# A table of priorities found offline, last rows kept in the score banks, last sums in two steps, and early memory denominators in a fused attention and MLP kernel

## The chip, the cores and the metric

The kernel runs on one core of one Trainium2 chip. The metric is the device time of one execution in microseconds (us), as the median of several runs. The profile of one execution is also at hand. In before its span, from the first to the last instruction, was 274.2 us, 1.7 us shorter than the device time of that same execution (275.94). A run is called slow here when it is over 1.5% above the fastest run of the same kernel.

## The reference, cut to what matters

```python
x = A_x                                   # (1, 2048, 512), bf16
xn = layernorm(x)
return x + A(xn, wq, wk, wv, wo, beta) + B(xn, w1, w2)

def B(x, w1, w2):                         # 512 -> 1792 -> 512
    return silu(x @ w1) @ w2

def A(x, wq, wk, wv, wo, beta):           # 32 heads of 16, 4 segments of 512 rows
    q, k, v = ...                         # split into heads and segments
    g = sigmoid(beta)
    M, z = 0, 0
    for s in range(4):
        p = softmax(qs @ ks.T * scale + causal_mask)
        a_dot = p @ vs
        pq = phi(qs)                      # phi(t) = t + 1 if t > 0 else exp(t)
        a_mem = (pq @ M) / (pq @ z + 1e-6)
        outs.append(g * a_mem + (1 - g) * a_dot)
        pk = phi(ks)
        M, z = M + pk.T @ vs, z + sum(pk)
    return concat(outs) @ wo
```

Two things can be divided late. A probability row is divided by its sum after it has been multiplied by the values, and `a_mem` is divided by its own denominator. In this kernel both kinds of denominator travel: they are gathered into a small tile, inverted by VectorE, written to DRAM, and read back as a full "replica" tile that VectorE multiplies with.

## The kernel before

The kernel is written as a plan. Each operation has an engine, a duration, a latency, dependencies and a due time, all in nanoseconds. A list scheduler, run while the kernel is built, simulates the five engines with these durations. The order that it finds is the order in which each engine gets its instructions.

```python
def op(self, eng, occ, lat, fn, due, r=(), w=(), kind="", take=None, ...):
    ...                                     # o.due = due, written by hand: tau(n) = T0 + n * PER
# in schedule(): per engine, the ready operation with the smallest key
key = -1e9 if o.kind in ("S",) else o.due   # score tiles first, then by due time
if o.kind == "PV" and lastS:
    key = -1e8
```

The first loads are such operations too. Their latency is a constant, whatever else is moving:

```python
load([("wk",)], ld_w("wk", "A_wk"), 2, 4000)      # keys, function, due, latency
load([("wq",)], ld_w("wq", "A_wq"), 3, 5000)
load([("wv",)], ld_w("wv", "A_wv"), 4, 6000)
load([("w1",)], ld_w("w1", "B_w1"), 5, 11000)
...
load([("w2",)], ld_w("w2", "B_w2"), 8, 16500)
```

Attention has 4 segments of 4 groups of 8 heads, and 5 score tiles for each group. That makes 80 score tiles, which all pass through one tile of four banks:

```python
for dt in range(DT):                        # 4 groups in a segment
    for q in range(5):
        op("PE", 222, 215, sc, tau(n) - 700, ..., w=[("psS", n)], kind="S")     # scores into psS
        op("ACT", 1757, 170, ex, tau(n) - 5000, r=[("psS", n)], w=[("Pt", n, 0)], kind="exp")
        op("POOL", ..., mask, ...)          # causal mask
    pvo = op("PE", 1090, 215, pv, tau(n0 + 8), ..., kind="PV")                   # probabilities x values
    ...                                     # evictions, row sums to zf, merge of two halves
```

At the end of each segment one `norm` handles the denominators of all four groups and of the memory together, and `out` makes the rows. Each row tile takes 14 matmuls with `w2`, evicted by VectorE together with x, then 4 with `wo`, evicted again. These groups share four banks `psb` with everything except the scores.

```python
def rc(K):                                  # after the sums of all 4 groups have landed
    K.nc.vector.reciprocal(out=K.rec32[lo:P, :], in_=K.zf[i2][lo:P, :])
    K.nc.vector.tensor_scalar(out=K.rec[i2][lo:P, :], in0=K.rec32[lo:P, :], scalar1=K.gcol[lo:P, 0:1], ...)
```

The softmax here doesn't subtract the row's maximum and nothing guards it: scores larger than these inputs give would overflow.

Of the kernel before, what the change touches and what calls it, by code (L numbers as in the profile page):

```python
# [9 lines left out]
ALU = mybir.AluOpType  # L10
# [21 lines left out]
PER = 2450  # L32
NB = 4
WARM = 60

RING = dict(
    xnT=2, kT=6, kTo=6, qT=6, phiK=1, phiQ=6, V=6, Pt=8, th=2, N=5, No=2, oT=4,
    zf=2, rec=2, rep=6, x=3, ek=3, phiKT=2, xn=2, pq=2, at=2, mv=4, rstd=4, zc=2,
    Mbf=2, zden=2, xa=4, stats=3, psS=1, drec=4, M32=1, z32=1,
# [12 lines left out]

def mm_ns(n):
    return n / 2.4 + 2.6


class Op:
    __slots__ = (
        "eng", "occ", "lat", "deps", "fn", "due", "kind", "take", "free", "mode",
        "start", "done", "bank", "n", "nleft", "outs", "hold", "not_before", "soft", "after",  # L60
    )


class Plan:

    def __init__(self):
        self.ops = []
        self.acc = {}
        self.build()
        self.link()  # L70
        self.schedule()

    def op(self, eng, occ, lat, fn, due, r=(), w=(), kind="", take=None, free=(), mode="F",
           deps=(), hold=0, not_before=0, after=()):
        o = Op()
        o.eng, o.occ, o.lat, o.fn, o.due, o.kind = eng, occ, lat, fn, due, kind
        o.take, o.free, o.mode = take, free, mode
        o.hold, o.not_before = hold, not_before
        o.deps = set(deps)
        o.n = len(self.ops)  # L80
        o.after = after
        o.outs = []
        o.start = o.done = None
        for k in r:
            self.acc.setdefault(k, ([], []))[0].append(o)
        for k in w:
            self.acc.setdefault(k, ([], []))[1].append(o)
        self.ops.append(o)
        return o
# [53 lines left out]
    def gemm(self, name, n, lhsT, rhs, due, r, ncol=L, extra=0):  # L143
        t = {}
        last = None
        for i in range(n):
            def fn(K, i=i):
# [6 lines left out]
                deps=[last] if last else (),  # L154
# [3 lines left out]
    def build(self):  # L158
# [24 lines left out]
        load([("wk",)], ld_w("wk", "A_wk"), 2, 4000)  # L183
        load([("wq",)], ld_w("wq", "A_wq"), 3, 5000)
        load([("wv",)], ld_w("wv", "A_wv"), 4, 6000)
        load([("w1",)], ld_w("w1", "B_w1"), 5, 11000)
        load([("x", 1, 0)], ld_x(1, 0), 6, 11500)
        load([("x", 1, 1)], ld_x(1, 1), 7, 12000)
        load([("w2",)], ld_w("w2", "B_w2"), 8, 16500)
        load([("wo",)], ld_w("wo", "A_wo"), 9, 17500)  # L190

        def beta(K):
            for r0, r1, ap in ((0, 64, [[0, 2], [1, 32], [1, 1]]), (64, P, [[1, 32], [0, 2], [1, 1]])):
                K.nc.sync.dma_start(
                    out=K.bcol[r0:r1, :],
                    in_=bass.AP(tensor=K.A_beta.tensor, offset=K.A_beta.offset, ap=ap),
                )
        op("SP", 1050, 2300, beta, 30000, w=[("bcol",)], kind="load", not_before=14000)
        for s in range(2, NSEG):
            for h in range(2):  # L200
                load([("x", s, h)], ld_x(s, h), 40000 + 1000 * s + h, 2600, nb=16000)
# [3 lines left out]
        def lnc(K):  # L205
            K.nc.gpsimd.memset(K.lnc[:, :, 0:1], EPS)
            K.nc.gpsimd.memset(K.lnc[:, :, 1:2], -0.5)
# [15 lines left out]
        def bmask(K):  # L223
# [12 lines left out]
            K.nc.gpsimd.memset(K.half[0:64, :], 0.5)  # L236
            K.nc.gpsimd.memset(K.half[64:128, :], -0.5)
            K.nc.gpsimd.memset(K.z32[:], 0.0)
        op("POOL", 2200, 150, bmask, 35000, w=[("bmask",), ("half",)], not_before=16000)

        def gate(K):
            K.nc.scalar.activation(out=K.gcol[:], in_=K.bcol[:], func=AF.Tanh, scale=K.half[:, 0:1])
            K.nc.vector.tensor_scalar(
                out=K.gcol[:], in0=K.gcol[:], scalar1=1.0, scalar2=None, op0=ALU.add
            )
        op("ACT", 300, 400, gate, 36000, r=[("bcol",), ("half",)], w=[("gcol",)])
# [22 lines left out]
    def ln(self, s, tau):  # L269
        op = self.op  # L270
        base = 1000 if s == 0 else (tau(1) if s == 1 else tau(20 * (s - 1) - 8))
        for j in range(TPS):
# [6 lines left out]
            op("DVE", 662, 150, stats, base + 700 * j, r=[("x", s, j // 2)],  # L279
               w=[("mv", s, j), ("stats", t)])  # L280
        step = 2 if s else 2
        for h in range(0, TPS, step):
            def rstd(K, h=h):
                t0 = s * TPS + h
                rs = K.rstd[:, t0 : t0 + step, :]
                K.nc.gpsimd.tensor_tensor(
                    out=rs, in0=K.mv[:, t0 : t0 + step, 1:2], in1=K.lnc[:, 0:step, 0:1], op=ALU.add
                )
                K.nc.gpsimd.tensor_tensor(out=rs, in0=rs, in1=K.lnc[:, 0:step, 1:2], op=ALU.pow)
            op("POOL", 770, 150, rstd, base + 1500 + 700 * h,  # L290
               r=[("mv", s, h + i) for i in range(step)] + [("lnc",)], w=[("rstd", s, h // step)])
        for j in range(TPS):
            t = s * TPS + j

            def norm(K, j=j, t=t):
# [5 lines left out]
            op("DVE", 300, 130, norm, base + 2000 + 700 * j,  # L301
               r=[("x", s, j // 2), ("mv", s, j), ("rstd", s, j // step)], w=[("xn", t)])
            if s == 0:
# [9 lines left out]
                op("PE", 420, 215, tr, base + 2500 + 700 * j, r=[("xn", t), ("ident",)],  # L313
# [18 lines left out]
    def proj(self, s, tau):  # L332
# [4 lines left out]
        for dt in range(DT):  # L337
            due = tau(20 * s + 5 * dt) - 3500
# [14 lines left out]
            op("POOL", 655, 130, odd, due + 1800, r=[("kT", 4 * s + dt), ("pm",)], w=[("kTo", 4 * s + dt)])  # L353
            if s < NSEG - 1:
# [4 lines left out]
                    tau(20 * s + 5 * dt + 4), lambda K, dt=dt: K.zc[i2][:, dt : dt + 1],  # L359
# [7 lines left out]
                op("SP", 1220, 2200, trk, tau(20 * s + 5 * dt + 6), r=[("phiKT", g)],  # L367
# [10 lines left out]
            if s > 0:  # L378
# [3 lines left out]
                    tau(20 * s + 2 + 2 * dt), None, [],  # L382
                )
        for j in range(TPS):
            due = tau(20 * s + 6) - 3500 + 100 * j
# [12 lines left out]
    def phi(self, s, dt, skey, src, dkey, dst, due, acc, extra):  # L398
# [19 lines left out]
        op("DVE", 690 if acc else 605, 140, st, due, r=[skey, ("ek", g, 1), ("ek", g, 0)],  # L418
           w=[dkey] + extra)

    def w1(self, s, tau):
# [3 lines left out]
        for ft in range(FT):  # L425
            g = s * FT + ft
            due = tau(2 + g * 74 / 56)
# [19 lines left out]
    def attend(self, s, tau):  # L447
# [9 lines left out]
        def p_ap(K, n0, par, g, kt):  # L457
            pt = lambda q: K.Pt[(n0 + q) % RING["Pt"]]
# [6 lines left out]
        for dt in range(DT):  # L465
            n0 = 20 * s + 5 * dt
            for q in range(5):
                n = n0 + q
# [14 lines left out]
                op("PE", 222, 215, sc, tau(n) - 700,  # L483
# [7 lines left out]
                op("ACT", 1757, 170, ex, tau(n) - 5000, r=[("psS", n)], w=[("Pt", n, 0)], kind="exp")  # L491
# [14 lines left out]
                op("POOL", 1180 if q in (1, 3, 4) else 590, 130, mask, tau(n) + 3500,  # L506
# [4 lines left out]
            def pv(K, dt=dt, tk=tk, n0=n0):  # L511
                for par in (1, 0):
                    for kt in (0, 1, 3, 2):
                        for g in range(4):
# [5 lines left out]
                                rhs=p_ap(K, n0, par, g, kt),  # L520
# [3 lines left out]
            keys = [("Pt", n0 + q, b) for q in range(5) for b in range(2)]  # L524
            pvo = op("PE", 1090, 215, pv, tau(n0 + 8), r=keys + [("V", 4 * s + j) for j in range(TPS)]
                     + [("ones", (4 * s + j) % RING["V"]) for j in range(TPS)], w=[("PV", s, dt)], take=list(tk), mode="C", kind="PV")
# [6 lines left out]
            def eve(K, tk=tk, nN=nN):  # L533
                K.nc.vector.tensor_copy(out=K.N[nN][:], in_=K.bank(tk[0])[:, :])
            due = tau(n0 + 9)
            op("DVE", 600, 135, evo, due, r=[("PV", s, dt)], w=[("No", g4)], free=[tk[1]])
            op("DVE", 600, 135, eve, due + 1, r=[("PV", s, dt)], w=[("N", g4, 0)], free=[tk[0]])
            for par in (1, 0):
                def sums(K, dt=dt, par=par, nN=nN, nNo=nNo):
                    src = K.No[nNo] if par else K.N[nN]  # L540
                    z0 = 16 * (1 - par)
                    for b in range(2):
                        r = 64 + 16 * dt + 2 * par + b
                        K.nc.sync.dma_start(
                            out=K.zf[i2][r : r + 13 : 4, :],
# [3 lines left out]
                   r=[("No", g4)] if par else [("N", g4, 0)], w=[("zf", s, 1 + par, dt)] + (  # L549
                       [] if par else [("Nsum", g4)]))  # L550

            def merge(K, nN=nN, nNo=nNo):
                for g in range(4):
                    K.nc.sync.dma_start(
                        out=K.N[nN][32 * g + 16 : 32 * g + 32, :],
                        in_=K.No[nNo][32 * g + 16 : 32 * g + 32, :],
                    )
            op("SP", 2300, 2100, merge, due + 2000, r=[("No", g4), ("N", g4, 0), ("Nsum", g4)],
               w=[("N", g4, 1)])

    def den(self, s, tau):
# [4 lines left out]
        def dn(K):  # L566
            for dt in range(DT):
                for b in range(2):
                    K.nc.tensor.matmul(
                        K.bank(tk)[32 * b : 32 * b + 32, 0:256],  # L570
                        lhsT=K.zden[i2][:, dt, :], rhs=K.phiQ[(4 * s + dt) % RING["phiQ"]][:, 256 * b : 256 * b + 256],
                        start=(dt == 0), stop=(dt == DT - 1), tile_position=(0, 32 * b),
                        skip_group_check=True,
                    )
        op("PE", 440, 215, dn, tau(20 * s + 11), r=[("phiQ", 4 * s + dt) for dt in range(DT)]
           + [("zden", s)], w=[("psD", s)], take=[tk], mode="C")

        def ev(K):
            K.nc.vector.tensor_scalar(
                out=K.zf[i2][0:64, :], in0=K.bank(tk)[0:64, 0:256], scalar1=1e-6, scalar2=None,  # L580
                op0=ALU.add,
            )
        op("DVE", 330, 135, ev, tau(20 * s + 11.5), r=[("psD", s)], w=[("zf", s, 0, 0)], free=[tk])

    def mem(self, s, tau):
# [4 lines left out]
        for dt in range(DT):  # L590
# [10 lines left out]
            last = op("PE", 230, 215, mm, tau(20 * s + 24),  # L601
# [10 lines left out]
        op("DVE", 610, 140, ev, tau(20 * s + 24.5), w=[("M32", s)], deps=[last], free=[tk])  # L612
# [357 lines left out]
```

## Time and profile before

| | before |
|---|---|
| median of 4 runs | 278.13 us (276.05 to 280.38, the last a slow run) |
| span of the profiled run, TensorE clock | 274.2 us, 0.944 |
| first exponential starts | 14.15 us |
| the 79 turns from the first exponential to the last | 230.31 us |
| from the end of the last exponential to the end | 27.9 us |

Here a "turn" is the time from the start of one exponential on ScalarE to the start of the next. The prediction below shows the lines for the table's last three rows. Two more views help to follow it. The first is SyncE's timeline of before, with the issues of the first loads (start, duration, queue, line, operation, output and input, count):

```profile
0.79 0.96 SPq L168 DMA_DIRECT2D x_all<-in_A_x_dram  x2
1.79 0.47 SPq L176 DMA_DIRECT2D wk<-in_A_wk_dram  x1
2.31 0.51 SPq L176 DMA_DIRECT2D wq<-in_A_wq_dram  x1
...
7.49 9.13 SPq L176 DMA_DIRECT2D wo<-in_A_wo_dram  x1
```

The reader sees that `wk` and `wq` are issued straight after the first half of x. The second view is TensorE's timeline of before around its longest turn, which starts at 34.71 us:

```profile
36.64 0.40 PE L477 MATMUL psS<-qT__104,kT__92 16*128 16x384 bf16 x8
...
49.60 0.38 PE L148 MATMUL psb__195<-w,hT__147 128*128 128x512 bf16 x1
49.91 0.40 PE L515 MATMUL psb__194<-Pt__129,V__123 128*32 128x512 bf16 x4
```

After the score tile at 36.64, TensorE works almost without a pause through projections and `w1` and `w2` groups until 49.91. Only then does the probabilities-times-values group read `Pt__129`, the buffer that the next exponential must overwrite. So the next exponential, at 50.36, stood back for 13.8 us after the end of the last one (36.59), although its score tile was ready. The values group had nothing to wait for: its last value tile was written at 22.3 and its last probability tile was masked at 29.5. It ran at 49.91 because the order had put it there.

### The profile page before, as it was taken

The numbers are of one execution on the slowest core, as the hardware profiler recorded it, in microseconds if no ns is written. First come the engines' busy times: TensorE is split into PE (matmuls) and PEld (weight loads), VectorE is DVE, ScalarE is ACT, GpSimd is POOL, SyncE is SP. The second block draws the span as 40 slices with busy tenths as digits, with TensorE's granted clock in tenths as the row PEclk, the third lists the DMA queues.
The fourth block names the chain that finished last, engine by engine and source line by source line (L and its number), as shares of the span: only waits on it lengthen the run. The fifth ranks groups of instructions, "written<-read, shape, count | busy, mean of one in ns | idle before, by whom it ended". The sixth has DMA issues, their size and how long they took to land.

```text
span 274.2 us, 4983 instructions
## 1 busy us (share of the span) xinstructions
PE 228.6 (83%) x1857; PEld 97.7 (36%) x1888; DVE 177.2 (65%) x309; ACT 193.1 (70%) x164; POOL 124.0 (45%) x213
## 2 busy tenths in 40 slices
PE   7796799999999989799999867999996279992054
PEld 7332234543443344334334432443342023441011
DVE  4797989944555997648458779932277485224174
ACT  1297686679899998887896887677979757770000
POOL 3385674245764644765543354734433424330000
PEclk9999999999999999999999988999999669998559
DMA  6999103220210013154200031110000311100132
GB/s 207 386 350 207 39 2 64 52 52 10 23 30 2 1 36 96 33 115 103 49 5 3 20 124 44 59 32 12 0 3 21 112 55 47 43 10 4 54 116 79
DMA packets 29130, 18.52 MB, mean 68 GB/s; under 512 B 15346, under 2 KB 28594, under 8 KB 29106
## 3 DMA queue, kind: packets, MB, share of 16 engines
q1 hardware_dynamic: 29106, 18.20, 24.5%
q8 instruction: 15, 0.25, 0.4%
q14 instruction: 9, 0.07, 0.1%
HBM read 11.53 MB, written 2.33 MB: 51 GB/s over the span
## 4 chain that ended last, share of the span: by engine, by line
PE 47%; DVE 15%; ACT 13%; DMA 10%; issue 8%; SPq 4%; POOL 2%; DVEq 0%; ACTq 0%; POOLq 0%
PE psb__197 L148 11%; PE psb__195 L148 10%; PE psb__194 L148 8%; PE psb__196 L148 7%; PE psS L477 6%; ACT Pt__129 L488 3%; DMA wv<-in_A_wv_dram 3%; DMA x_all<-in_A_x_dram 2%; PE psb__196 L515 2%; ACT th__158 L434 1%; PE psb__197 L515 1%; ACT Pt__134 L488 1%; PE psb__194 L515 1%; DVE rec L640 1%; DMA rep__176<-drec__201 1%
## 5 line engine op out<-in xcount | busy, mean ns | idle before, releaser
L148 PEld LDWEIGHTS <-w 128*128 128x128 bf16 x224 | 21.4, 99 | 32.2 <-issue 11.5
L488 ACT ACTIVATE Pt__129<-psS 128x2048 bf16<-128x2048 f32 x10 | 18.8, 1875 | 6.7 <-PE psS L477 3.6
L488 ACT ACTIVATE Pt__134<-psS 128x2048 bf16<-128x2048 f32 x10 | 18.8, 1877 | 6.6 <-PE psS L477 4.6
L488 ACT ACTIVATE Pt__136<-psS 128x2048 bf16<-128x2048 f32 x10 | 18.8, 1880 | 5.8 <-PE psS L477 5.0
L488 ACT ACTIVATE Pt__133<-psS 128x2048 bf16<-128x2048 f32 x10 | 18.8, 1879 | 5.1 <-PE psS L477 4.2
L488 ACT ACTIVATE Pt__135<-psS 128x2048 bf16<-128x2048 f32 x10 | 18.8, 1875 | 3.7 <-PE psS L477 3.5
L488 ACT ACTIVATE Pt__131<-psS 128x2048 bf16<-128x2048 f32 x10 | 18.8, 1879 | 3.5 <-PE psS L477 3.3
L488 ACT ACTIVATE Pt__132<-psS 128x2048 bf16<-128x2048 f32 x10 | 18.8, 1877 | 3.2 <-PE psS L477 3.1
L488 ACT ACTIVATE Pt__130<-psS 128x2048 bf16<-128x2048 f32 x10 | 18.8, 1877 | 2.4 <-PE psS L477 2.2
L502 POOL TENSOR_SCALAR_AFFINE_SELECT Pt__129<-Pt__129 128x512 bf16<-128x512 bf16 (+1 forms) x14 | 10.7, 780 | 13.9 <-ACT Pt__129 L488 13.9
L502 POOL TENSOR_SCALAR_AFFINE_SELECT Pt__133<-Pt__133 128x512 bf16<-128x512 bf16 (+1 forms) x14 | 10.2, 746 | 11.9 <-ACT Pt__133 L488 11.9
L502 POOL TENSOR_SCALAR_AFFINE_SELECT Pt__136<-Pt__136 128x512 bf16<-128x512 bf16 (+1 forms) x14 | 9.6, 702 | 12.9 <-ACT Pt__136 L488 12.9
L502 POOL TENSOR_SCALAR_AFFINE_SELECT Pt__132<-Pt__132 128x512 bf16<-128x512 bf16 (+1 forms) x14 | 10.4, 759 | 10.7 <-ACT Pt__132 L488 10.7
L502 POOL TENSOR_SCALAR_AFFINE_SELECT Pt__135<-Pt__135 128x512 bf16<-128x512 bf16 (+1 forms) x14 | 10.0, 724 | 11.4 <-ACT Pt__135 L488 11.4
L502 POOL TENSOR_SCALAR_AFFINE_SELECT Pt__131<-Pt__131 128x512 bf16<-128x512 bf16 (+1 forms) x14 | 9.6, 701 | 10.4 <-ACT Pt__131 L488 10.4
L502 POOL TENSOR_SCALAR_AFFINE_SELECT Pt__134<-Pt__134 128x512 bf16<-128x512 bf16 (+1 forms) x14 | 9.8, 714 | 8.6 <-ACT Pt__134 L488 8.6
L502 POOL TENSOR_SCALAR_AFFINE_SELECT Pt__130<-Pt__130 128x512 bf16<-128x512 bf16 (+1 forms) x14 | 9.7, 707 | 8.5 <-ACT Pt__130 L488 8.5
L148 PE MATMUL psb__196<-xnT__89,w 128*128 128x512 bf16 x36 | 9.6, 379 | 4.0 <-DVE hT__139 L440 2.1
L148 PE MATMUL psb__196<-pq__181,Mbf__190 128*128 128x512 bf16 x2 | 1.2, 608 | 12.1 <-DVE pq__181 L683 12.1
L148 PEld LDWEIGHTS <-wk 128*128 128x128 bf16 x80 | 7.4, 98 | 10.5 <-issue 3.6
L148 PEld LDWEIGHTS <-wq 128*128 128x128 bf16 x80 | 7.2, 97 | 9.6 <-issue 2.7
L148 PE MATMUL psb__194<-xnT__90,w 128*128 128x512 bf16 x36 | 10.3, 408 | 0.0
(601 smaller groups left out, 654.0 us busy)
## 6 DMA issues: line engine op xcount, KB each, us to landing
w<-in_B_w_dram SPq DMA_DIRECT2D x2, 1792.0 KB
x_all<-in_A_x_dram SPq DMA_DIRECT2D x8, 256.0 KB
out_dram<-x_all SPq DMA_DIRECT2D x16, 128.0 KB
wk<-in_A_wk_dram SPq DMA_DIRECT2D x1, 512.0 KB
wq<-in_A_wq_dram SPq DMA_DIRECT2D x1, 512.0 KB
wv<-in_A_wv_dram SPq DMA_DIRECT2D x1, 512.0 KB
wo<-in_A_wo_dram SPq DMA_DIRECT2D x1, 512.0 KB
rep__175<-drec__198 SPq DMA_DIRECT2D x2, 128.0 KB
```

The costliest lines, as they stand in the source:

```text
L148: K.nc.tensor.matmul(K.bank(t)[:, 0:ncol], lhsT=lhsT(K, i), rhs=rhs(K, i), start=(i == 0), stop=(i == n - 1),)
L434: K.nc.scalar.activation(out=K.th[g % RING["th"]][:], in_=K.bank(t)[:, :], func=AF.Tanh, scale=0.5)
L477: K.nc.tensor.matmul(K.psS[:, g, c : c + nq], lhsT=kk[r0:r1, kt * P : (kt + 1) * P], rhs=K.qT[b][r0:r1, kt * P : L], start=True, stop=True ...
L488: K.nc.scalar.activation(out=K.Pt[n % RING["Pt"]][:], in_=K.psS[:], func=AF.Exp, scale=SCALE)
L502: K.nc.gpsimd.affine_select(out=a, in_=a, compare_op=ALU.is_ge, fill=0.0, base=0, pattern=[[0, a.shape[1]], [1, P]], channel_multiplier=-1,)
L515: K.nc.tensor.matmul(K.bank(tk[par])[32 * g : 32 * g + 32, kt * P : L], lhsT=K.V[(4 * s + kt) % RING["V"]][:, 4 * dt + g, par : par + 2, : ...
L640: K.nc.vector.reciprocal(out=K.rec32[lo:P, :], in_=K.zf[i2][lo:P, :])
```

## The change

The intent is to replace the hand-written due times by a table. It has 1064 integers, one for each operation or matmul group, found by a search outside the kernel that ran the same scheduler on the duration model. At the same time four details change: some durations, the last rows, the sums of the last segment, and the time at which memory denominators are made. The list scheduler itself changes too, which the cut below does not show: it now keeps two of the four banks free for a probabilities-times-values group that is ready and nearly due, and the hand-written due times become the formula `DUE`.

```diff
-PER = 2450
+PER = 2400
+DUE = dict(ln=[10.99, 5.7, 21.46, 26.84], kq=[-13.26, ...], ...)   # a formula, used only without the table
+PRIO = [
+    -223886, -213142, 63705, 177752, 22538, 11838, 1323, ...        # 1064 entries, cut
+]
 # op():
+        o.due = int(PRIO[unit] if PRIO else due)

 # attend(): the last group's tiles in another order, its values group in two halves
+            end = s == NSEG - 1 and dt == DT - 1
+            qs = (4, 0, 1, 3, 2) if end else range(5)
-                op("ACT", 1757, 170, ex, ...)
+                op("ACT", 1770, 178, ex, ...)
+            halves = [((1,), (4, 0, 1)), ((0,), (4, 3, 2))] if end else [((1, 0), range(5))]

 # sums of the last segment: groups 0 to 2 in one step, group 3 in another
+            dts = range(DT) if s < NSEG - 1 else ([3] if dt == 3 else [0, 1, 2])
+                K.nc.vector.reciprocal(out=K.zr[0:nr, :], in_=zt[0:nr, :])

 # den(): memory denominators inverted and multiplied into phi(q) at once, not at the segment's end
+            K.nc.vector.reciprocal(out=K.zf[:], in_=K.zf[:])
+                    out=k[:], in0=k[:], in1=K.mrep[dt % RING["mrep"]][:], op=ALU.mult

 # out(): the last four row tiles each stay in one bank of the score tile until they are done
+        seq = [(ident2, x)] + [(hT[i], w2[i]) ...] + [(oT[i], wo[i]) for 3 groups] + [(oTm, wo[3]), (oT[3], wo[3])]
+                K.nc.tensor.matmul(K.psO[j][:, :], lhsT=a(K), rhs=b(K), start=(i == 0), stop=(i == len(seq) - 1))
```

In the last rows x itself comes in through TensorE, with a doubled identity as the weight (`ident2`; the eviction halves the sum). The memory part of the last group (`oTm`) and its attention part are multiplied with `wo` apart, so the memory part need not wait.

The diff does not show one effect: the loads are operations like the others, so the table also reorders the queue of the first ten loads.

## The prediction

> **What bounds the kernel now.** I read the page first (busy shares, slices), then ScalarE's timeline, then the stretches after the last exponential, then the chain of waits of the first 30 us.
>
> ```profile
> PE 228.6 (83%) x1857; PEld 97.7 (36%) x1888; DVE 177.2 (65%) x309; ACT 193.1 (70%) x164; POOL 124.0 (45%) x213
> ...
> PEclk9999999999999999999999988999999669998559
> ```
>
> No engine is full on average, and TensorE's granted clock falls in a few slices late in the run. So the average does not name the bound, and I go to the timeline of ScalarE. Columns: start, duration, engine, line, operation, then the idle time before it and its releaser.
>
> ```profile
> 14.15 1.88 ACT L488 ACTIVATE Pt__129<-psS 128x2048 bf16<-128x2048 f32 x1 [0.65 <-PE psS L477]
> ...
> 34.71 1.88 ACT L488 ACTIVATE Pt__136<-psS 128x2048 bf16<-128x2048 f32 x1 [1.04 <-PE psS L477]
> ...
> 50.36 1.88 ACT L488 ACTIVATE Pt__129<-psS 128x2048 bf16<-128x2048 f32 x1 [1.69 <-PE psb__194 L515]
> ...
> 242.00 1.88 ACT L488 ACTIVATE Pt__135<-psS 128x2048 bf16<-128x2048 f32 x1 [0.56 <-PE psS L477]
> 244.46 1.88 ACT L488 ACTIVATE Pt__136<-psS 128x2048 bf16<-128x2048 f32 x1 [0.58 <-PE psS L477]
> ```
>
> There is one score tile psS, so score matmuls and exponential take turns: a turn is 244.46 - 242.00 = 2.46 us, at best about 2.43. Eighty turns stand between 14.15 and 244.46: 79 intervals took 230.3 us, against 79 x 2.43 = 192. The 38 us above that are turns in which the next score tile came late, the worst from 34.71 to 50.36 (15.65 us). This alternating chain is the spine.
>
> After the last exponential (ends at 246.3) comes a tail to 274.2:
>
> ```profile
> 252.32 1.75 DVE L640 RECIPROCAL rec<-zf__171 128x256 f32<-128x256 bf16 x1 [2.87 <-DMA zf__171<-N__159]
> ...
> 260.27 0.42 DVE L683 TENSOR_TENSOR pq__181<-phiQ__112,rep__176 128x512 bf16<-128x512 bf16 x1 [5.81 <-DMA rep__176<-drec__201]
> ```
>
> ```profile
> 252.00:256.00 4.00, 0.00 (x0) 0.00 (x0) 2.11 (x2) 0.00 (x0) 0.00 (x0) 0.50 0.08 18
> 256.00:260.00 4.00, 0.00 (x0) 0.00 (x0) 0.00 (x0) 0.00 (x0) 0.00 (x0) 0.50 0.19 56
> ```
>
> The last two lines are stretches (busy us of PE, PEld, DVE, ACT, POOL, then clock, DMA share, GB/s): TensorE does nothing for 12 us while row sums travel to a reciprocal and back, and its clock falls to 0.50.
>
> The start hangs on the weight loads, here in the chain of waits (start, us, what):
>
> ```profile
> 2.86 7.26 DMA wv<-in_A_wv_dram
> ...
> 19.66 5.84 DMA x_all<-in_A_x_dram
> ```
>
> wv lands at 10.12. A later x load of the same queue, 0.26 MB, needs 5.84 us because w2 and wo are still moving before it.
>
> **What the Trainium skill says.** "DMA: Bandwidth & Descriptors", section "Queues, rings and completion order": SyncE's transfers use one row of rings, and on each DMA engine "descriptors are consumed in ring order". The trace agrees: by windows of 1 us, 2.6 MB had moved by 10.12 us, and x's first half, wk, wq and wv, issued first, are 2.10 MB. "TensorE: Matmul & The Clock Gate", section "What's actually happening": after an idle window TensorE runs at half clock until it has been busy a while. It agrees: clock 0.50 from 252 to 268 us, and 512-column matmuls start 0.43 us apart at 265.75, 0.216 apart by 269. "Perfetto Trace Analysis", section "Identifying the Most-Contended Engine": matmul busy share is a poor measure of distance to the roofline; here 83% busy hides both the late turns and the tail.
>
> **The change part by part.**
>
> *Table of priorities.* It sets the order of every engine's instructions, so I counted the new program's order. Between two score tiles TensorE needs 0.49 us for the score tile, 0.216 for each 512-column matmul and 1.16 for a probability-times-value group: nine matmuls and a tile are 2.43, as the timeline shows, and a group, five matmuls and a tile made 237.13 - 234.39 = 2.74. ScalarE needs 2.43 with at most one small activation beside the exponential (14.15 to 16.53), and about 1.77 + 0.05 + 0.5 each with more (two took 81.70 - 78.97 = 2.73). The larger of the two, summed over 79 intervals, gives 204.0 us for the new order; TensorE's parts alone sum to 197.5, ScalarE's to 197.8. The longest interval is 3.3 us; the 57-matmul lump behind the 15.65 us is gone. The same count of the old order gives 235.0, less 14.9 in three places where a run of activations and a run of matmuls lie side by side though the count adds them: 220.1. The trace took 230.3, so 10.2 us were stalls that the count does not see (late evictions, loads, replicas). The new order was made with durations nearer the trace (exponential 1770 where it was 1757, LayerNorm statistics 794 for 662), so I charge 6 us: chain 210, down 20.3.
>
> *The same table moves the loads.* This I did not expect. The new queue order is x four times, w1, wv, wk, w2, wq, wo; the old was x twice, wk, wq, wv, w1, and so on. The plan gives each load a fixed delay after its issue, whatever lies before it, so moving wq back behind w2 costs it nothing. On the chip I expect it to cost. Sizes are those of the DMA view: x 1.05 MB, w1 1.83, wv 0.52, wk 0.52, w2 1.83, wq 0.52. wk is done when 3.93 MB have moved, wq when 6.29 have. Before, the moved bytes reached these at 13.35 and 20.05 us; with 1.35 us more, as wv needed beyond its own bytes, wk is usable at 14.7 and wq at 21.4. TensorE's order is transposes, k, q, k, score tile, so it stands idle from 9.6 to 14.7 and again until 21.4, and restarts at half clock: eight matmuls at 0.43 are 3.4 us. First score tile at 24.8, first exponential at 25.4, where it was 14.15: up 11.2.
>
> *Memory denominators early, sums in two steps, last rows in the score banks.* Nothing but moved work until the tail: the fourfold column tiling of the denominators and eight added matmuls (doubled identity, oTm) are under 2 us of TensorE and lie in the count. In the tail, let E be the end of the last exponential. TensorE: mask 0.64, second half of the group 0.6, start E + 1.4 with small gaps; 79 matmuls of 512 columns follow it, 79 x 0.216 = 17.1, so it ends at E + 18.5. The chain of the last sums: ScalarE copy to E + 2.2, sums landed E + 4.4 (in before 2.1 us from issue), reciprocal 1.75 and scaling 0.35 to E + 6.7, but SyncE's four merge issues (2.44) hold the write until E + 7.6, landed E + 9.8, replica 2.8 more, multiply 0.42: E + 13.1. Its first consumer is the 60th of the 79 matmuls, E + 14.1. So the chain hides by about 1 us, and matmuls bound the tail. Eviction 0.7 and store 2.7 as at the end of before: end E + 22.0. From the start of the last exponential that is 23.9, where before took 274.2 - 244.46 = 29.7: down 5.8. (The same work also leaves the part before E, which the count of 204 includes.)
>
> Sum: + 11.2 - 20.3 - 5.8 = - 14.9; 277.69 - 14.9 = 262.8 us.
>
> **The rivals.** *Loads land as the plan thinks.* If the transfers shared the engines evenly, wq would come near 14 us and the chain start almost as before: about 252 us. The 5.84 us of the late x load speak against it. *A plan without slack.* Everything is in order on each engine and four banks are shared, so a late VectorE operation passes its delay on. The plan has 640 ns for the phi step, and the trace has some at 967; VectorE's 177 us would be three quarters of a shorter span. If such stalls make 16 us and not 6, the result is 273, a bare 2% gain. Against it: stretches of the old order ran turn after turn at 2.44. *The last sums bind the tail.* If the write or replica is 3 us later, TensorE waits 2 us and may lose clock: 265.
>
> **Range and chances.** The two large uncertain terms are the start (0 to 12 us) and the stalls (2 to 16 us). Full loss of both is 273, none of the start loss 252; I take 251 to 273. Faster by over 2% means under 272.1: 0.86. Within 2%: 0.11. Slower: 0.03, as the stalls would have to pass 26 us.
>
> **What would show it.** First exponential near 25 us, TensorE idle up to 21 us waiting for wq. 79 turns in about 210 us with none above 6 us. From the last exponential's end about 22 us, TensorE unbroken at full clock for 17 of them. Wrong if the first exponential starts before 18 us, if turns average over 2.8 us, or if TensorE idles over 2 us in the tail for the last replica.

## The result, and the profile after

| | before | predicted | after |
|---|---|---|---|
| median | 278.13 us | 262.8 us | 256.22 us (254.88 to 258.69, 4 runs) |
| span of the profiled run, clock | 274.2 us, 0.944 | 259.3 us | 253.2 us, 0.973 |
| first exponential starts | 14.15 | 25.4 | 25.20 |
| 79 turns | 230.31 | 210 | 203.76 |
| end of the last exponential to the end | 27.9 | 22.0 | 22.36 |
| turns of 3.5 us or more | 7 | none above 6 us | 3 (longest 4.57) |

The verdict is faster, with a ratio of 0.9245 (95% interval 0.9143 to 0.9347; before's slow run is left out). A ratio here is always the mean time of one kernel's fast runs over the mean of the other's fast runs of the same rounds, so it is not quite the ratio of the medians quoted. The predicted span of 259.3 is 25.4 + 210 + 1.9 for the last exponential + 22.0.

The page of after, busy times and the granted clock in 40 slices:

```profile
PE 224.4 (89%) x1887; PEld 96.9 (38%) x1920; DVE 178.2 (70%) x308; ACT 194.5 (77%) x170; POOL 130.0 (51%) x231
...
PEclk9955999999999999999999999999999999999999
```

Busy times are within 6 us of before on every engine: the work is nearly the same, and it is mainly its placing that changed. The dent in the clock has moved from the end to the start.

**The start.** SyncE's timeline of after shows the new queue order:

```profile
0.79 1.99 SPq L296 DMA_DIRECT2D x_all<-in_A_x_dram  x4
2.82 0.47 SPq L304 DMA_DIRECT2D w<-in_B_w_dram  x1
3.33 0.51 SPq L304 DMA_DIRECT2D wv<-in_A_wv_dram  x1
3.88 0.51 SPq L304 DMA_DIRECT2D wk<-in_A_wk_dram  x1
4.43 2.68 SPq L304 DMA_DIRECT2D w<-in_B_w_dram  x1
7.16 6.01 SPq L304 DMA_DIRECT2D wq<-in_A_wq_dram  x1
```

TensorE's timeline of after shows what it costs (in brackets: idle time before, and what ended it):

```profile
14.23 0.61 PE L276 MATMUL psb__201<-xnT__88,wk 128*128 128x512 bf16 x1 [4.47 <-DMA wk<-in_A_wk_dram]
...
21.01 1.89 PE L276 MATMUL psb__202<-xnT__88,wq 128*128 128x512 bf16 x4 [4.90 <-DMA wq<-in_A_wq_dram]
22.69 1.91 PE L276 MATMUL psb__203<-xnT__88,wk 128*128 128x512 bf16 x4
24.54 0.61 PE L609 MATMUL psS<-qT__102,kTo__96 32*128 32x512 bf16 x4
```

And ScalarE's timeline of after has the first exponential:

```profile
25.20 1.88 ACT L620 ACTIVATE Pt__128<-psS 128x2048 bf16<-128x2048 f32 x1 [7.63 <-PE psS L609]
```

TensorE stands until 14.23 for `wk`, then until 21.01 for `wq`. It then runs its four matmuls in 1.9 us, because it starts at half clock. The windows of after say the same (window, length, then busy us and count of PE, weight loads, DVE, ACT, POOL, then clock, DMA share, GB/s):

```profile
12.00:16.00 4.00, 1.55 (x3) 0.43 (x4) 0.00 (x0) 0.00 (x0) 0.00 (x0) 0.50 1.10 348
16.00:20.00 4.00, 0.11 (x1) 0.00 (x0) 0.69 (x1) 0.63 (x1) 1.27 (x2) 0.50 1.10 348
```

The DMA share stands above 1 in both windows, while TensorE does 1.55 + 0.11 = 1.66 us of work in 8. The start is bound by transfers.

**The turns.** The distribution of turns moved as the change intended:

| kernel | under 2.6 us | 2.6 to 3.5 | 3.5 and more | sum of all above 2.43 us each |
|---|---|---|---|---|
| before | 47 | 25 | 7 (longest 15.65) | 38.3 us |
| after | 59 | 17 | 3 (longest 4.57) | 11.8 us |

The seven long turns of before held 26.7 us of excess; the three of after hold 5.1. One of the three, the turn of 4.27 us from 169.64 to 173.91, comes from the early memory denominators. The chain of waits of after has, at that time (start, us, what):

```profile
168.84 3.09 DMA mrep__177<-dmem__199
```

VectorE stands 0.93 and 0.66 us for two such replicas, with the evictions behind them, and the matmul ahead of the next score tile waits for one of those evictions (172.42 to 173.11).

**The tail.** VectorE's timeline of after, from the second reciprocal on:

```profile
235.47 1.74 DVE L705 RECIPROCAL zr<-zf 16x256 f32<-16x256 bf16 x1 [2.74 <-DMA zf<-N__158]
...
244.13 0.42 DVE L843 TENSOR_TENSOR oT__168<-N__158,rep__181 128x512 bf16<-128x512 bf16 x1 [1.67 <-DMA rep__181<-drec__196]
```

TensorE's timeline of after, the first and the last matmul that read this tile:

```profile
245.24 0.38 PE L929 MATMUL psO__2919<-wo,oT__168 128*128 128x512 bf16 x1
...
249.34 0.38 PE L929 MATMUL psO__2921<-wo,oT__168 128*128 128x512 bf16 x1
```

The windows of after from the last exponential on:

```profile
231.00:240.00 9.00, 8.84 (x54) 3.97 (x54) 4.05 (x7) 1.18 (x2) 0.53 (x1) 1.00 0.17 55
240.00:250.00 10.00, 9.67 (x45) 4.21 (x43) 3.83 (x7) 0.84 (x2) 0.00 (x0) 1.00 0.16 55
```

The last multiply ends at 244.55, and the first matmul that reads it starts at 245.24 with no idle time before it. TensorE is busy for 18.5 of 19 us at full clock, where the prediction showed before's windows with none at all. The tail is now bound by matmuls.

### The profile page after: what moved, and what is told of

The parts are those of the page before. It is cut to its first block, busy times and chain, and to the rows that moved or that the text cites. A ratio compares the mean times of both kernels' runs of the same rounds, so it can differ in the third digit from the quotient of the medians.

```text
span 253.2 us, 5054 instructions
## 1 busy us (share of the span) xinstructions
PE 224.4 (89%) x1887; PEld 96.9 (38%) x1920; DVE 178.2 (70%) x308; ACT 194.5 (77%) x170; POOL 130.0 (51%) x231
## 4 chain that ended last, share of the span: by engine, by line
PE 38%; ACT 16%; DVE 16%; POOL 9%; DMA 9%; issue 6%; SPq 3%; DVEq 0%; ACTq 0%; POOLq 0%
PE psb__201 L276 6%; PE psb__204 L276 6%; PE psb__202 L276 6%; DMA wq<-in_A_wq_dram 5%; PE psb__203 L276 5%; PE psS L609 5%; ACT Pt__133 L620 2%; ACT Pt__129 L620 2%; ACT Pt__131 L620 2%; PE psO__2920 L929 2%; PE psO__2921 L929 2%; PE psO__2918 L929 2%; PE psO__2919 L929 2%; SPq L304 2%; ACT Pt__130 L620 2%
## 5 line engine op out<-in xcount | busy, mean ns | idle before, releaser
L276 PEld LDWEIGHTS <-w 128*128 128x128 bf16 x224 | 20.4, 98 | 26.3 <-issue 6.6
L276 PE MATMUL psb__201<-xnT__89,w 128*128 128x512 bf16 x44 | 11.7, 380 | 0.1
L276 PEld LDWEIGHTS <-wk 128*128 128x128 bf16 x64 | 6.3, 103 | 12.9 <-DMA wk<-in_A_wk_dram 4.6
L276 PE MATMUL psb__203<-xnT__88,w 128*128 128x512 bf16 x32 | 8.9, 379 | 2.5 <-DVE hT__140 L570 1.5
L276 PEld LDWEIGHTS <-wq 128*128 128x128 bf16 x64 | 5.8, 100 | 13.1 <-DMA wq<-in_A_wq_dram 5.8
L938 ACT ACTIVATE x_all<-psO__2919 128x512 bf16<-128x512 f32 x1 | 0.6, 597 | 12.5 <-PE psO__2919 L929 12.5
```

The source lines that it names most:

```text
L276: K.nc.tensor.matmul(K.bank(t)[:, 0:ncol], lhsT=lhsT(K, i), rhs=rhs(K, i), start=(i == 0), stop=(i == n - 1),)
L938: K.nc.scalar.activation(out=K.x_all[:, t_ % XT, :], in_=K.psO[j][:, :], func=AF.Copy, scale=0.5)
```

## The experiments

Nine kernels ran, all correct. The first four shared their rounds with before on one chip, as did the next four; the ninth ran alone with before. In the first session one of e1's four runs was slow (252.52), and so were three of before's seven; the record calls the verdicts of e1 to e4 unclear, although the intervals of e1, e2 and e3 lie wholly beyond 2%. Before's median in these three sessions was 278.42, 278.54 and 278.74 us, so the tables can be read together. All columns after the ratio are from the profiled run, in us. In after, e5 and e6 the loads stand in the same order, and their first exponentials still differ by 1 us (25.20, 26.19 and 25.79), so less than that at the start is no finding.

| run | median (range) | ratio to before [95%] | first exponential | 79 turns | end of last exponential to end |
|---|---|---|---|---|---|
| after | 256.22 (254.88 to 258.69) | 0.9245 [0.9143, 0.9347] | 25.20 | 203.76 | 22.36 |
| e1 loads old | 248.3 (247.24 to 252.52); fast runs 247.91 | 0.8928 [0.8801, 0.9055] | 13.75 | 208.02 | 23.35 |
| e2 before, loads new | 290.33 (287.95 to 291.31) | 1.0457 [1.035, 1.0564] | 26.07 | 229.5 | 28.7 |
| e3 no table | 253.82 (252.17 to 255.94) | 0.9157 [0.9051, 0.9263] | 13.64 | 212.43 | 24.95 |
| e4 before, rows | 277.99 (277.16 to 278.86) | 1.0025 [0.9932, 1.0118] | 14.07 | 232.4 | 28.75 |
| e5 merge on ScalarE | 255.36 (254.74 to 256.54) | 0.9189 [0.9132, 0.9246] | 26.19 | 203.53 | 22.30 |
| e6 merge twice | 259.45 (258.98 to 260.64) | 0.9337 [0.928, 0.9394] | 25.79 | 205.41 | 24.22 |
| e7 loads old, gate late | 244.92 (243.62 to 247.2) | 0.8813 [0.8729, 0.8897] | 13.39 | 206.17 | 22.36 |
| e8 wq before w2 | 250.49 (249.64 to 251.98) | 0.9014 [0.8954, 0.9075] | 20.70 | 203.43 | 22.29 |
| e9 x before w1 | 243.45 (242.93 to 245.85) | 0.8739 [0.8699, 0.8779] | 15.52 | 203.36 | 22.34 |

### e1: the changed kernel with the first ten loads in the old order

```diff
     plan = Plan()
+    loads = [o for o in plan.order if o.kind == "load"][:10]
+    for o, f in zip(loads, [o.fn for o in sorted(loads, key=lambda o: o.n)]):
+        o.fn = f
```

> The changed kernel, nothing moved but the ten first loads, which go back to the old queue order (x, wk, wq, wv, w1, x, w2, wo). Theory L (the table's load order delays the start by what must move before wq): first exponential near 14.2 us where the changed kernel has 25.2, the 79 turns unchanged at 204 +- 3 us, tail 22.4, span 242 to 244, time 244 to 247, some 10.5 us under the changed kernel. Rival S (the rest of the table was planned with loads where they are, so the time won at the start is lost again in turns waiting for w1 or the second x): turns 209 to 214 us and time 250 to 256.

The first exponential came at 13.75, so 11.45 us came back, as the theory of the load queue has it. The median of the fast runs is 247.91, a gain of 8.3 and not of 11: the 79 turns took 208.02 us, 4.3 more, and the tail 1.0 more (a replica of the last segment's sums took 4.73 us there, and TensorE stood 0.61 for it). The turns lie between what the two theories had, 201 to 207 and 209 to 214. ScalarE's timeline of e1 shows where, in the turn from 18.51 to 25.78:

```profile
18.51 1.88 ACT L620 ACTIVATE Pt__130<-psS 128x2048 bf16<-128x2048 f32 x1
25.01 0.20 ACT L375 ACTIVATE gcol<-bcol 64x1 f32<-64x1 bf16 x1 [4.62 <-DMA bcol<-in_A_beta_dram]
...
25.78 1.86 ACT L620 ACTIVATE Pt__131<-psS 128x2048 bf16<-128x2048 f32 x1
```

The gate, sigmoid of beta, stands after the third exponential in ScalarE's order. In after it came at 31.89 and waited for nothing. With the chain starting 11 us earlier it stood before its load: ScalarE was idle for 4.62 us, and the next exponential, which follows the gate in its order, came only at 25.78. This was a wait that neither theory had named, and e7 tests it.

### e2: the kernel before with the new order of loads

```diff
+    loads = [o for o in plan.order if o.kind == "load"][:10]
+    fns = [o.fn for o in loads]
+    for o, i in zip(loads, (0, 1, 7, 6, 5, 4, 2, 8, 3, 9)):
+        o.fn = fns[i]
```

> The kernel before with only the new queue order of the ten loads. Theory L: first matmul waits for wv to 12.9, and q for wq to about 21.2; first exponential near 25 us where it was 14.15, and the time goes up by 8 to 11 us, to 286 to 289 us (a little may be given back, because the old order has later waits for x and w1 in its first turns). Rival (slack of the old order swallows it): up by less than 4 us.

TensorE's timeline of e2:

```profile
21.88 1.89 PE L148 MATMUL psb__196<-xnT__89,wq 128*128 128x512 bf16 x4 [4.78 <-DMA wq<-in_A_wq_dram]
```

The first exponential moved from 14.15 to 26.07, which is 11.9 us, and the time rose by as much: 290.33 - 278.42 = 11.9, a little more than the 8 to 11 expected. The turns stayed as they were (229.5 for 230.31). The order of loads costs the same 11 to 12 us in a kernel that has nothing else of the change.

### e3: the changed kernel without its table

```diff
-PRIO = [ ... ]
+PRIO = []          # due times from the formula DUE; this also puts the loads in the old order
```

> The changed kernel with the table emptied, so that the order comes from the hand formula of due times in the same file; loads are then in the old order. Same count as in the prediction: turns 210.7 us (one interval of 7.9, two of 3.8). Theory L: first exponential near 14.2; if stalls are 0 to 6 us, last exponential starts at 225 to 231, span 249 to 255, time 252 to 258: the table's shorter turns (204) are worth less than its late start costs, so this is no slower than the changed kernel. Rival T (the table is what makes the gain): turns over 222 us, time over 264.

The table as shipped is not shown to be worth anything: 253.82 without it and 256.22 with it, with overlapping intervals. The rows of the table above say why. Without the priorities the start is 11.6 us earlier (13.64), the turns are 8.7 us longer (212.43) and the tail 2.6 longer (24.95). A comparison with the late load taken out is e7 against e3: 244.92 against 253.82, with disjoint intervals of the ratios, so the table's order is worth 8.9 us once the loads and the gate are taken out of its hands. And e3 is some 24 us faster than before, with a start as early and no table: its turns are 17.9 us shorter and its tail 2.9. That part comes from the rest of the change (scheduler, formula, durations, sums, rows), which no run here takes apart. One turn makes most of the difference in turns. ScalarE's timeline of e3:

```profile
141.62 1.88 ACT L527 ACTIVATE Pt__129<-psS 128x2048 bf16<-128x2048 f32 x1 [0.79 <-PE psS L516]
...
151.49 1.88 ACT L527 ACTIVATE Pt__130<-psS 128x2048 bf16<-128x2048 f32 x1
```

That is one turn of 9.87 us; the longest with the table is 4.57. It is again work in an unlucky order on TensorE, but not the wait of before's 15.65 us turn. Here the score tile itself came late: TensorE first did 13 matmuls of other work, four for k and a values group, the four for q came only at 148.29, VectorE evicted them from 150.20, and the tile followed at 150.98.

### e4: the kernel before with the last rows kept in the score banks

```diff
 # cut and shortened. out(), last segment only: one group per row tile in psO[j] = a score bank
+            if s == NSEG - 1:
+                self.rows(s, j, w2l, wol, tau(20 * s + 30) + 1000 * j)
+                continue
+    def rows(...):                  # ident2 x, 14 w2, 4 wo; half of the evictions on ScalarE
 # the pool of psS is closed before the pool of psO opens
```

> The kernel before with only the last four output rows put whole into the score banks after the last exponential (doubled identity for x, 14 w2 and 4 wo matmuls in one group, half of them evicted by ScalarE). If turns bind before the last exponential and the sums after it, the last exponential stays near 244.5 us (the last ten turns are 2.44 with or without nine w2 matmuls in each), and TensorE fills the first 14 us of the tail but still waits for the replicas of all four groups: tail 27 instead of 27.9 and time within 1% of before, 275 to 278. Rival (w2 matmuls bound those turns, or moving 56 of them shortens the tail by itself): 266 to 270.

No gain: 1.0025, and the turns grew from 230.31 to 232.4. ScalarE's timeline of e4 shows the last turns:

```profile
243.80 1.88 ACT L489 ACTIVATE Pt__136<-psS 128x2048 bf16<-128x2048 f32 x1 [0.78 <-PE psS L478]
246.47 1.88 ACT L489 ACTIVATE Pt__137<-psS 128x2048 bf16<-128x2048 f32 x1 [0.79 <-PE psS L478]
```

The 56 `w2` matmuls that used to fill the last turns now wait for the score banks. The turns don't get shorter for it, at 2.66 us each: between 242 and 248 us the windows have TensorE busy for 1.23 us of 6 at a clock of 0.50, and a score tile takes 0.64 us. And after the last exponential the chain of waits still ends on the replicas:

```profile
262.86 3.18 DMA rep__176<-drec__201
...
266.08 3.45 DMA rep__177<-drec__201
```

The rows are only a place to put work under a wait, for all denominators of the segment together, and that wait did not get shorter. In this run it even began later. VectorE's timeline of e4 has the last group's first eviction, with which the sums start:

```profile
252.78 0.69 DVE L532 CAST No__166<-psb__195 128x512 bf16<-128x512 f32 x1 [14.40 <-PE psb__195 L516]
```

That is 4.4 us after the end of the last exponential, against 1.8 in before (248.16), because seven matmuls of the rows, at half clock, stand ahead of the values group. So e4 shows that the rows as built here gain nothing. With the values group first they might take some 1.7 us off the tail (an estimate: the 2.6 us of later start less the 0.9 us by which the tail grew); no run shows it. In after similar rows stand with sums in two steps.

### e5: the last group's four merge transfers issued by ScalarE

```diff
-                    K.nc.sync.dma_start(out=K.N[nN][r : r + 16, :], in_=K.No[nNo][r : r + 16, :])
+                    (K.nc.scalar if end else K.nc.sync).dma_start(out=K.N[nN][r : r + 16, :], in_=K.No[nNo][r : r + 16, :])
```

> The changed kernel with the four merge transfers of the last group issued by ScalarE instead of SyncE, which takes them out of the way of the last sums' write: the last replica should land about 2 us earlier. Theory P (79 matmuls bind the tail and hide the sums): last exponential to end stays 22.4 +- 0.4, time unchanged within 1 us. Rival C (the last sums bind): tail 20.5.

VectorE's timeline of e5, the last multiply:

```profile
243.68 0.42 DVE L843 TENSOR_TENSOR oT__168<-N__158,rep__181 128x512 bf16<-128x512 bf16 x1 [0.45 <-DMA rep__181<-drec__196]
```

TensorE's timeline of e5, its first reader:

```profile
246.00 0.38 PE L929 MATMUL psO__2919<-wo,oT__168 128*128 128x512 bf16 x1
```

From the last multiply's end, at 244.10, to its first reader the room is 1.9 us now, where it was 0.7. The tail stayed at 22.30. Counted from the end of the last exponential, the multiply starts 1.2 us earlier than in after (12.1 for 13.3), not 2 as expected. So the chain of the last sums does not bind the tail in after.

### e6: those four merges issued twice

```diff
-                for g in range(4):
+                for g in [0, 1, 2, 3] * (2 if end else 1):
```

> The changed kernel with the four merge transfers of the last group issued twice on SyncE, which puts the last sums' write some 2.5 to 3 us later. Theory P: the hidden chain had 0.7 us to spare (multiply done 244.55, its first matmul 245.24), so TensorE now waits 1.8 to 2.4 us at that matmul and the tail is 24.3 to 24.8; time up by about 2. If the chain had more slack than read: no change.

TensorE's timeline of e6:

```profile
249.41 0.39 PE L929 MATMUL psO__2919<-wo,oT__168 128*128 128x512 bf16 x1 [1.76 <-DVE oT__168 L843]
```

The same matmul now stands 1.76 us for VectorE, and the tail grew by 1.86, to 24.22. Together e5 and e6 bracket the room. A shorter chain gives nothing. Four more issues (2.44 us by the prediction's row) less the room of 0.7 make 1.7, about what was lost. The median is up by 3.2, more than the 2 expected: in the profiled run the first exponential came 0.6 us later and the turns took 1.65 more, in a stretch that the edit doesn't touch. In one of these turns the early replica took 4.23 us where after's took 3.09; why, no run shows.

### e7: e1 with the gate's activations moved later

```diff
     # e1's lines, then
+    gate = plan.acc[("gcol",)][1][0]
+    user = min(plan.acc[("gcol",)][0], key=lambda o: o.start)
+    plan.order.remove(gate)
+    plan.order.insert(next(i for i, o in enumerate(plan.order) if o.start >= user.start - 8000), gate)
```

> The run with the old load order, and the three small activations on beta (the gate) moved from before the fourth exponential to some 8 us before their first use. Theory: the fourth turn of that run (7.27 us) was ScalarE standing 4.6 us before the gate, whose beta load came last in the queue, and the sixth (4.11) was TensorE at half clock after that stop. Without it both turns are 2.4 to 2.8: first exponential 13.8, chain 202 to 203, tail 22.4, span 240 to 242, time 241 to 244. Rival (the fourth turn really waited for x or w1 behind it): the turns stay long, 247 to 249.

244.92, that is 3.0 us less than e1's fast runs (247.91), and the turn that had taken 7.27 us takes 2.38 here. So the wait for beta was real. It fell slightly short of the 241 to 244 expected, for two reasons that the trace shows. x's second half waits behind `w1` in the old load order, in the chain of waits of e7:

```profile
4.16 12.31 DMA x_all<-in_A_x_dram
```

Its LayerNorm starts at 16.49, VectorE is crowded after that, and turns 5 to 7 (counted by the exponential that ends them) took 2.99, 3.23 and 3.87 us. And the gate's three additions on GpSimd, now at 68 us, lie in a turn that took 4.73 us where after has 3.54.

### e8: the changed kernel with only wq moved ahead of w2

```diff
+    loads = [o for o in plan.order if o.kind == "load"][:10]
+    fns = [o.fn for o in loads]
+    for o, i in zip(loads, (0, 1, 2, 3, 4, 5, 6, 8, 7, 9)):
+        o.fn = fns[i]
```

> The changed kernel with one swap in its load order, wq ahead of w2. By bytes moved: wq is complete after 4.46 MB, 14.8 us, plus 1.35: usable at 16.2 where the changed kernel has 21.0. First score tile 3.5 us after that, first exponential at 20.2 (25.2 in the changed kernel), turns 204, tail 22.4: span 248, time 251. Rival (the start is not set by the bytes ahead of wq, but by the number of loads or by the w1 load): first exponential stays within 1.5 us of 25.2.

TensorE's timeline of e8:

```profile
15.16 0.61 PE L276 MATMUL psb__201<-xnT__88,wk 128*128 128x512 bf16 x1 [5.78 <-DMA wk<-in_A_wk_dram]
...
16.84 1.91 PE L276 MATMUL psb__202<-xnT__88,wq 128*128 128x512 bf16 x4
```

`wq` is there when TensorE comes to it. The first exponential starts at 20.70 (expected 20.2), and the median is 250.49, 5.7 us less than after. This is a dose between after and e1: 25.20, 20.70 and 13.75 us for the first exponential. The 1.83 MB of `w2` ahead of `wq` cost 4.5 us. The rest goes with `wk`, which still stands behind `w1` and is usable only at 15.16, with TensorE idle before it and at half clock after.

### e9: all of x ahead of w1, and the gate before the 13th exponential

```diff
+    loads = [o for o in plan.order if o.kind == "load"][:10]
+    fns = [o.fn for o in sorted(loads, key=lambda o: o.n)]      # x, x, wk, wq, wv, w1, x, x, w2, wo
+    for o, i in zip(loads, (0, 1, 2, 3, 4, 6, 7, 5, 8, 9)):
+        o.fn = fns[i]
+    gate = plan.acc[("gcol",)][1][0]
+    plan.order.remove(gate)
+    exps = [o for o in plan.order if o.kind == "exp"]
+    plan.order.insert(plan.order.index(exps[12]), gate)
```

> The changed kernel with loads x, wk, wq, wv, second x, w1, w2, wo and the gate before the thirteenth exponential. In the run with the late gate the second x was waited for until 16.46 us and VectorE's backlog made turns 5 to 7 long (2.99, 3.23, 3.87), and the gate's small POOL operations at 68 us made turn 23 1.2 us longer than in the changed kernel. By bytes the second x is now in after 2.62 MB (10.2 + 1.35 = 11.5 us), w1 after 4.46 MB (16.2), just before its first matmul near 16.7. First exponential 13.4, turns 203 to 204, tail 22.4: span 240 to 242, time 241 to 243.5. Rival (w1 becomes the wait instead): a turn near 17 us over 4 us and no gain on 244.9.

The median of 6 runs is 243.45, below both kernels. In the profiled run the first exponential came at 15.52 and not at 13.4. The windows of e9 say why:

```profile
12.00:16.00 4.00, 4.00 (x15) 1.32 (x14) 2.14 (x4) 1.11 (x2) 1.27 (x2) 0.65 1.03 387
```

TensorE is busy without a gap, but at a clock of 0.65: the first projections ran at half clock, where e7, with the same loads ahead of them, ran them at full clock (four q matmuls in 1.03 us against 1.91). The three groups ahead of the first score tile (k, q, k) took from 10.70 to 15.07, 4.4 us, where e7's took from 10.27 to 12.95, 2.7 us. So 1.7 of the 2.1 us that this start is behind e7's are the clock; no load is waited for. It need not be a cost of this order: four of the six runs have a mean clock of 1.0 and spans of 241.2 to 242.0 us, where the profiled run has 0.993 and 243.1. The turns gave 2.8 us back against e7 (203.36 for 206.17), as the earlier x and the earlier gate should (the turn with the gate's additions in e7, 4.73, is 3.55 here); the two edits were not run apart. e9 and e7 are not clearly apart: their intervals overlap between 0.8729 and 0.8779.

**Not tested.** The early memory denominators, the new durations, the scheduler's new rule for banks, the formula and the sums in two steps were not tried alone. Their shares are open.

## Why the prediction was right, and where its size was off

The median of 256.22 lies in the range of 251 to 273 and on the side given 0.86, but 6.6 us below the point. By the prediction's own terms:

| term | predicted | measured | measured less predicted |
|---|---|---|---|
| first exponential | 25.4 | 25.20 | -0.2 |
| 79 turns | 204.0 + 6 of stalls | 203.76 | -6.2 |
| tail from the end of the last exponential | 22.0 | 22.36 | +0.4 |
| median less span | 3.5 | 3.0 | -0.5 |

The last line compares 277.69 - 274.2 with 256.22 - 253.2. The four add up to -6.5, the miss but for rounding.

**The start was right, in mechanism and size.** `wk` was usable at 14.23 (14.7 predicted) and `wq` at 21.01 (21.4), and TensorE restarted at half clock. e2 put the same loss of 11.9 us into the old kernel, e1 took 11.45 us out of the new one, and e8 took out a part. The rival that loads land as the plan thinks is dead: `wq` was 7 us past the time that this rival had. One line held against that rival was read too strongly, though. By windows of 1 us the bytes of `w2` and `wo` had moved by about 21.7 us in before, and the late x load landed only at 25.50; what made the rest of its 5.84 us is not shown.

**The step that was mis-sized is the charge of 6 us for stalls.** The prediction summed, for each turn, the larger of TensorE's and ScalarE's work, got 204.0, and added stalls "so I charge 6 us". The trace took 203.76 in all. Laid turn by turn beside the count, some turns are 5.5 us longer in sum and others 5.7 us shorter, a net of -0.2. No view prints these two sums; a recount from the trace, where some matmul records are missing, gives a count of 201.6 with 6.2 longer and 4.1 shorter. So stalls of about the charged size were there, such as the 4.27 us turn behind the replica. The count has slack of about the same size, though. That the two nearly cancel was not foreseen, and that the total fell on 204 is partly luck. A likely reason, which no run tests: a larger-of-two in every turn takes it that a long turn of matmuls and the next long turn of activations can't overlap, but neighbours can lend to each other through the buffers between them. The prediction had seen this in the old order, where it took 14.9 us off the count, and left it out for the new one. The rival of a plan without slack, with 16 us of stalls, did not come about; neither did single long turns like e3's or before's, once the table had spread the lumps.

**The tail was right.** The matmuls bind it: unbroken at clock 1.00, with 0.7 us of room where 1 us was predicted. e5 and e6 show both sides of that room. e4 adds what the prediction didn't have: the rows put into before, without the sums in two steps, gained nothing as they were built.

**What the prediction did not ask.** It said that the table's moved loads cost 11.2 us, but not whether the table pays for them. It hardly does: e3 without any table is as fast within its interval. The plan gave each load a constant latency, so the search was free to move `wq` behind `w2`. With x and the three small weights ahead of `w1` and `w2`, and the gate off its early place, the same table runs at 243.45 (e9), which is 0.8739 of before, against 0.9245 as shipped.

## What to carry to other kernels

A search over a duration model can use a flaw of the model: where the model gives a transfer a constant latency, the search may put a needed load behind a large one, so model the queue by its bytes or pin the first loads by hand. Estimate a chain of alternating engines by the sum of the larger part in each turn, but a charge for stalls goes with a credit for what neighbouring turns can lend each other; the two were of about the same size. When the start of an in-order kernel moves earlier, look for the next instruction whose own load has not moved with it.

## What the Trainium skill lacked or had wrong

- "DMA: Bandwidth & Descriptors", section "Queues, rings and completion order", gives the order of a ring but no delay from a load's last byte to its use; the fixed cost per DMA elsewhere on that page is fitted for transfers issued by GpSimd. In these runs, by windows of 1 us, a large load was usable about 1.0 to 1.3 us after the moved bytes had reached the end of its own place in the queue: before's wv at 10.12 us, after's wk at 14.23 and wq at 21.01. A small transfer behind large ones came later: e1's beta, a few hundred bytes, landed at 25.65, which is 3.88 us after its last issue and some 3 us after the loads ahead of it had moved.
- The same page, section "Issuing engines are not separate DMA queues", calls the time that a sequencer needs to initiate a DMA "usually small relative to the DMA itself". Here the issue of wo held SyncE for 9.13 us in before, and that of wq for 6.01 us in after, while the loads ahead were moving, where the first issues took about 0.5 us; the 0.52 MB of wo themselves need about 1.5 us at the 345 to 350 GB/s of those windows. What SyncE has to issue next waits for that; why it is held, no run here shows.
- "VectorE: DVE Perf Modes" says that the reciprocal is an iterative divide with a repeat count of 8, but neither that page nor another one that I read gives a duration. It took 1.73 to 1.75 us for 256 columns, on 16, 48, 64 and 128 partitions alike, so joining rows on more partitions cost nothing here.
